# Attention probabilities of chunks 1 to 7 turned by DMA instead of TensorE

## Chip, cores and metric

One core of a Trainium2 chip runs the whole program. The metric is the device time of one execution in microseconds (us), as the median of several runs. A kernel is one launch; weights and inputs start in DRAM and the result ends in DRAM.

## The reference, cut to what matters

Attention over 4 batches x 8 heads (576 positions, 64 per head) feeds two feed-forward blocks one after the other. Four heads of a batch look at the last 32 positions, four at every 32nd position.

```python
scores = scale * q @ k.T                    # scale = 1/8
scores = where(mask[head], scores, -1e9)    # local heads: 0 <= q-k < 32; strided heads: q-k >= 0 and (q-k) % 32 == 0
attn = exp(scores - max(scores))
attn = attn / (sum(attn) + 1e-9)
x = (attn @ v), heads side by side          # 2304 tokens x 512
h = x @ moe_w_in;   x = (h * sigmoid(1.702 * h)) @ moe_w_out      # 512 -> 2048 -> 512
h = x @ moe2_w_in;  out = (h * sigmoid(h)) @ moe2_w_out
```

## The kernel before

**Order of work.** The engines' instruction streams are written out by a planner (class `Planner`, lines 62 to 180). Every piece of work is a task with a priority (a due time), an estimated cost for each engine that may do it, the tasks it follows and the buffers it takes. `Planner.run` plays the tasks through once at build time, giving each engine the ready task of lowest priority, and emits the instructions in that order. On the chip each engine then works through its own stream strictly in order, and waits where the plan was too early. A DMA task occupies SP for its issue; its data count as landed two us after a shared link, with 0.27 MB per us, has carried them (lines 171 to 173).

**Chunks.** The 2304 tokens are eight chunks of 288: a batch's first half (even chunks, `s = 0`) and second half (odd chunks, `s = 1`). `chunk(c)` (line 843) is the first feed-forward block: 16 tasks of 12 matmuls for `h` (line 862), then 16 of 12 for the output (line 893), each operand of chunks 1 to 7 being two fp16 parts, high and low, with three products for each pair. `attention(c, ...)` (line 565) is the attention of chunk c, and is planned into the feed-forward of chunk c-1: its tasks have due times between those of that chunk's matmuls, and the chunk's output `x1` must be ready when `chunk(c)` begins. Chunk 7's feed-forward and the second block follow in a second plan (lines 961 to 1334).

**Attention of one chunk.** `pair(i)`, i = 0 to 3 (line 632), does one local and one strided head. TensorE forms the scores with the queries on the partitions (line 669). VectorE takes the row maxima and subtracts them (678, 690), ScalarE takes the exponentials (698), VectorE the row sums and reciprocals (702, 715), and GpSimd multiplies (723), which leaves normalised fp32 probabilities: `sml`, 96 queries x 3 blocks x 128 keys, and `sms`, 72 x 4 x 72 in even chunks, 63 x 5 x 126 in odd ones. The product with V needs the keys on the partitions. TensorE transposes block by block into a PSUM bank (line 730: 3 blocks of `sml`, 4 or 5 of `sms`), then two evictions leave the two fp16 parts in `ptt`, scaled by `PSC` = 4096: the high part by ScalarE or VectorE (743, 745), the low part by VectorE (748). `times_v(pr)` (line 757) multiplies by V (780) for two heads at a time, in the order pr = 0, 2, 1, 3 (0 and 1 local, 2 and 3 strided), and lines 810 and 813 write `x1`. Chunk 0 works in fp32 and keeps one scaled fp32 copy in `ptt` (737).

**Buffers.** Eight PSUM banks (`ps`) serve everything; `sl` and `st` are four copies of `sml` and `sms`, `pt` six of `ptt`; `qh`, `vz` and `x1` exist once.

Of the kernel before, what the change touches and what calls it, by code (L numbers as in the profile page):

```python
# [22 lines left out]
PSC = 2.0 ** 12  # L23
# [160 lines left out]
def attention_moe_moe2_kernel(  # L184
# [146 lines left out]
    jk = at.tile([128, NK], BF16, name="jk")  # L331
    jv = at.tile([128, NK], BF16, name="jv")
# [23 lines left out]
    for i in range(2):  # L356
# [6 lines left out]
    nc.gpsimd.memset(vz[:, :, :, 1], 0.0)  # L363


    P = Planner({"ps": range(8), "rq": [0], "rk": range(2), "rv": [0], "qh": [0],
                 "k0": [0], "k1": [0], "vz": [0], "x1": [0], "sl": range(NSM), "st": range(NSM), "pt": range(NPT), "t": range(NTS),
# [6 lines left out]
    def act_t(n):  # L374
        return {"ACT": 0.17 + 0.00083 * n}
# [189 lines left out]
    def attention(c, b):  # L565
# [66 lines left out]
        def pair(i):  # L632
# [84 lines left out]

            for g in range(2):
# [3 lines left out]
                kno = P.add({"POOL": 0.25 + 0.0022 * nb * nk}, t + 8 + g, lambda on, g=g, smv=smv, nq=nq, nb=nb, nk=nk:  # L722
                            nc.gpsimd.tensor_tensor(  # L723
                                out=smv(), in0=smv(), in1=sus[0:nq, sl.idx, 3 * g:3 * g + nb, None].to_broadcast([nq, nb, nk]),
                                op=ALU.mult), [krc], (), [sl, st])
                p, pb = P.buf("ps"), P.buf("pt")
# [6 lines left out]
                if c == 0:  # L733
                    def evict(on, p=p, pb=pb, n=n, nk=nk):
                        o, x = ptt[0:nk, pb.idx].rearrange("p a n -> p (a n)").bitcast(F32)[:, 0:n], banks[p.idx][0:nk, 0:n]
                        if on == "ACT":
                            nc.scalar.activation(out=o, in_=x, func=AF.Copy, scale=PSC)
                        else:
                            nc.vector.tensor_scalar(out=o, in0=x, scalar1=PSC, scalar2=None, op0=ALU.mult)
                    kp = P.add({"DVE": 0.45} | act_t(n), t + 12 + g, evict, [ktr], [pb], [p])  # L740
                else:
                    kp = P.add(act_t(n) | {"DVE": 0.4}, t + 12 + g, lambda on, p=p, pb=pb, n=n, nk=nk:
# [14 lines left out]
        def times_v(pr):  # L757

            nq, nk, blocks = geom(s, pr >= 2)
            nb = len(blocks)  # L760
            t = b + tab["av"][pr % 2] + pr // 2
            pa = [P.buf("ps") for _ in range(1 if c else 2)]

# [639 lines left out]
```

## Time and profile before

| | |
|---|---|
| median of 3 runs | 878.31 us (874.52 to 879.46) |
| the profiled execution | 878.42 us, of which 876.6 us from its first to its last instruction |
| TensorE matmuls busy | 850.7 us (97% of the span) |
| VectorE / ScalarE / GpSimd busy | 694.1 / 537.5 / 417.3 us |
| chunks 1 to 7 of attention, with the feed-forward of chunks 0 to 6 around them | about 84 to 492 us of the span |

TensorE's matmuls overlap in the pipeline and their ends are modelled, so the cost of a group of matmuls in a stream is read as the distance from its start to the start of the next group, not as the sum of the durations. Idle time counts only on the engine that bounds a stretch. Lines such as L730 are lines of the kernel before.

### The profile page before, as it was taken

The numbers are of one execution on the slowest core, as the hardware profiler recorded it, in microseconds if no ns is written. First come the engines' busy times: TensorE is split into PE (matmuls) and PEld (weight loads), VectorE is DVE, ScalarE is ACT, GpSimd is POOL, SyncE is SP. The second block draws the span as 40 slices with busy tenths as digits, with TensorE's granted clock in tenths as the row PEclk, the third lists the DMA queues.
The fourth block names the chain that finished last, engine by engine and source line by source line (L and its number), as shares of the span: only waits on it lengthen the run. The fifth ranks groups of instructions, "written<-read, shape, count | busy, mean of one in ns | idle before, by whom it ended". The sixth has DMA issues, their size and how long they took to land.

```text
span 876.6 us, 21029 instructions
## 1 busy us (share of the span) xinstructions
PE 850.7 (97%) x8198; PEld 721.6 (82%) x8198; DVE 694.1 (79%) x1259; ACT 537.5 (61%) x1009; POOL 417.3 (48%) x432
## 2 busy tenths in 40 slices
PE   4999999899999999999999999999999999999997
PEld 3976768688888888878888888888888998888886
DVE  5769999989987799899577273789888799868742
ACT  5678568769869588697574334354555476646410
POOL 3657565554453465475323163677887552221110
PEclk9999999999999999999999999999999999999999
DMA  9948232268264375384300472576675898746501
GB/s 316 316 119 258 77 109 83 91 194 256 81 201 169 115 227 190 107 265 135 120 31 15 162 285 76 194 224 222 219 227 193 298 301 286 261 166 224 196 27 49
DMA packets 86083, 155.25 MB, mean 177 GB/s; under 512 B 8416, under 2 KB 45792, under 8 KB 84960
## 3 DMA queue, kind: packets, MB, share of 16 engines
q1 hardware_dynamic: 85984, 153.91, 53.6%
q8 instruction: 64, 1.05, 0.5%
q14 instruction: 35, 0.29, 0.1%
HBM read 100.40 MB, written 53.48 MB: 176 GB/s over the span
## 4 chain that ended last, share of the span: by engine, by line
PE 83%; DVE 9%; DMA 2%; issue 2%; POOL 1%; ACT 1%; SPq 0%; DVEq 0%; POOLq 0%
PE aps L1173 9%; PE aps L893 8%; PE aps L1284 8%; PE aps L862 7%; PE gps L893 5%; PE hps L1173 5%; PE gps L1173 4%; PE hps L1284 4%; PE gps L1284 4%; PE hps L893 3%; PE gps L862 3%; PE hps L862 3%; PE aps L859 2%; DMA tt<-g_scratch 2%; PE aps L669 2%
## 5 line engine op out<-in xcount | busy, mean ns | idle before, releaser
L1284 PEld LDWEIGHTS <-wf 128*128 128x128 f16 x1512 | 147.6, 98 | 19.5 <-issue 2.0
L1173 PEld LDWEIGHTS <-wf 128*128 128x128 f16 x1680 | 150.6, 98 | 15.3
L862 PEld LDWEIGHTS <-regA 128*128 128x128 f16 x1152 | 112.3, 98 | 28.7 <-issue 0.2
L893 PEld LDWEIGHTS <-regB 128*128 128x128 f16 x1152 | 108.5, 98 | 29.4 <-DVE sml L690 1.3
L989 POOL TENSOR_TENSOR tt<-tt 128x256 f32<-128x256 f32 (+2 forms) x84 | 74.7, 898 | 45.6 <-ACT tt L1185 13.4
L862 PE MATMUL aps<-x,regA 128*128 128x288 f16 x636 | 84.3, 286 | 0.0
L893 PE MATMUL aps<-g,regB 128*128 128x288 f16 x576 | 79.0, 289 | 1.7 <-DVE sml L690 1.2
L293 POOL TENSOR_TENSOR wm<-wm 128x512 int32<-128x512 int32 x32 | 45.8, 1430 | 60.9 <-DVE wm L288 47.1
L984 ACT ACTIVATE wf<-tt,xsg 128x512 f16<-128x512 f32 x87 | 58.0, 712 | 25.6 <-PE hps L1284 7.3
L996 DVE SCALAR_TENSOR_TENSOR wf<-tt,xsg,wf 128x512 f16<-128x512 f32 x87 | 71.4, 868 | 0.0
L723 POOL TENSOR_TENSOR sml<-sml,sus 96x384 f32<-96x384 f32 x32 | 30.3, 946 | 70.5 <-DVE sus L715 58.6
L1284 PE MATMUL aps<-regA,wf 128*128 128x256 f16 x456 | 53.2, 273 | 0.1
L1173 PE MATMUL aps<-xfa,wf 128*128 128x256 f16 (+1 forms) x528 | 53.1, 256 | 0.0
L893 PE MATMUL gps<-g,regB 128*128 128x288 f16 x336 | 45.7, 286 | 0.0
L1185 ACT ACTIVATE tt<-tt 128x512 f32<-128x512 f32 x39 | 24.4, 625 | 30.9 <-DVE tt L1180 29.5
L984 ACT ACTIVATE wf<-regB,xsg 128x512 f16<-128x512 f32 x39 | 26.8, 713 | 19.9 <-DMA regB<-g_scratch 7.4
L1173 PE MATMUL aps<-g,wf 128*128 128x256 f16 x324 | 38.8, 273 | 0.0
L1284 PE MATMUL aps<-regB,wf 128*128 128x256 f16 x312 | 37.0, 273 | 0.0
L862 PE MATMUL hps<-x,regA 128*128 128x288 f16 x264 | 35.6, 286 | 0.0
L723 POOL TENSOR_TENSOR sms<-sms,sus 72x288 f32<-72x288 f32 (+1 forms) x32 | 35.3, 1103 | 0.0
L862 PE MATMUL gps<-x,regA 128*128 128x288 f16 x252 | 34.2, 286 | 0.0
L1284 PE MATMUL hps<-regA,wf 128*128 128x256 f16 x264 | 32.4, 273 | 1.7 <-DVE x L1299 1.4
(350 smaller groups left out, 2098.1 us busy)
## 6 DMA issues: line engine op xcount, KB each, us to landing
tt<-g_scratch SPq DMA_DIRECT2D x76, 256.0 KB, 3.8
g_scratch<-tt SPq DMA_DIRECT2D x64, 256.0 KB, 3.0
w<-in_moe_w_out_dram SPq DMA_DIRECT2D x24, 512.0 KB, 4.3
rv<-in_v_dram SPq DMA_DIRECT2D x8, 1024.0 KB, 5.6
regB<-in_moe_w_in_dram SPq DMA_DIRECT2D x16, 512.0 KB, 8.8
w<-in_moe_w_in_dram SPq DMA_DIRECT2D x16, 512.0 KB, 3.7
w_scratch<-wm SPq DMA_DIRECT2D x32, 256.0 KB, 3.3
regB<-g_scratch SPq DMA_DIRECT2D x32, 256.0 KB, 3.8
```

The costliest lines, as they stand in the source:

```text
L293: nc.gpsimd.tensor_tensor(out=di, in0=m.bitcast(I32), in1=di, op=ALU.add)
L669: nc.tensor.matmul(x[0], lhsT=x[1], rhs=x[2], start=False, stop=x[3], skip_group_check=True)
L723: nc.gpsimd.tensor_tensor(out=smv(), in0=smv(), in1=sus[0:nq, sl.idx, 3 * g:3 * g + nb, None].to_broadcast([nq, nb, nk]), op=ALU.mult), [k ...
L859: nc.tensor.matmul(o, lhsT=w[:, kk, :], rhs=x1f[:, kk, :], start=(kk == 0), stop=(kk == KD - 1))
L862: nc.tensor.matmul(o, lhsT=pvA[:, f, x, kk, :], rhs=x1[:, y, kk, :], start=(i == 0), stop=(i == 3 * KD - 1))
L893: nc.tensor.matmul(o, lhsT=pvB[:, f, u, dt * 128:(dt + 1) * 128], rhs=g1[:, w, f, :], start=(f == 0 and j == 0), stop=(f == KF - 1 and j = ...
L984: nc.scalar.activation(out=out, in_=in_, func=AF.Copy, scale=s)
L989: return P.add({e: x for e, x in any_add(n).items() if e in by}, prio, lambda on: (nc.gpsimd if on == "POOL" else nc.vector).tensor_tensor ...
L996: dve_t(n), prio, lambda on: nc.vector.scalar_tensor_tensor(out=lo(), in0=src(), scalar=s(), in1=hi(), op0=ALU.mult, op1=ALU.subtract),
L1173: nc.tensor.matmul(place(b, f), lhsT=wf[:, nf * g + f, x, wa, 128 * kk:128 * kk + 128], rhs=rhs.rearrange("p (h t) -> p h t", h=2) if n2 = ...
L1185: return P.add(act_t(512), t + 5, lambda on: nc.scalar.activation(out=sl(b), in_=sl(b), func=AF.Silu), after, (), [b], tab="silu")
L1284: nc.tensor.matmul(bank(b)[:, 256 * half:256 * half + 256], lhsT=fb[:, x, a, 128 * f:128 * f + 128], rhs=wt[:, 4 * p + f, z, wi, :], start ...
```

## The change

For chunks 1 to 7, lines 723 to 750 are replaced. GpSimd first multiplies the reciprocals by `PSC` (one small instruction for each pair), then normalises as before. While the queries are still on the partitions, the high fp16 part is written by ScalarE or GpSimd and the low part, the difference, by VectorE or GpSimd, into `phl` (96 queries x 3 blocks x 2 parts x 128 columns) or `phs` (80 rows x 5 x 2 x 128). There is one buffer of each. Then one DMA transpose issued by SP for each of the two heads turns the whole buffer from SBUF to SBUF into `ptt`: 56 of them, 96 x 768 elements for a local head, 80 x 1024 or 64 x 1280 for a strided head (queries are rounded up to 16), 144 to 160 KiB each. The transposes on TensorE, their PSUM banks and both evictions fall away for these chunks. Chunk 0 keeps them. The layout of `ptt` and the slices that `times_v` reads are adapted. The targets `jk` and `jv` of the squares, whose contents nobody reads, become one byte wide, and `phs` is cleared once at the start by GpSimd.

```diff
-    NSM, NPT, NTS, NCV, NF = 4, 6, 4, 2, 8
+    NSM, NPT, NTS, NCV, NF, NHL = 4, 6, 4, 2, 8, 1
...
-    ptt = at.tile([128, NPT, 2, 316], F16, name="ptt")
+    ptt = at.tile([128, NPT, 640], F16, name="ptt")
+    phl = at.tile([LQ, NHL, NLB, 2, 128], F16, name="phl")
+    phs = at.tile([80, NHL, 5, 2, 128], F16, name="phs")
...
-    jk = at.tile([128, NK], BF16, name="jk")
-    jv = at.tile([128, NK], BF16, name="jv")
+    jk = at.tile([128, NK], mybir.dt.uint8, name="jk")
+    jv = at.tile([128, NK], mybir.dt.uint8, name="jv")
...
+    nc.gpsimd.memset(phs, 0.0)
...
+            kno = None
             for g in range(2):
...
-                kno = P.add({"POOL": 0.25 + 0.0022 * nb * nk}, t + 8 + g, ...
-                p, pb = P.buf("ps"), P.buf("pt")
+                def normalise(on, g=g, smv=smv, nq=nq, nb=nb, nk=nk):
+                    if c and g == 0:
+                        nc.gpsimd.tensor_scalar(out=sus[:, sl.idx, 0:n8], in0=sus[:, sl.idx, 0:n8], scalar1=PSC, scalar2=1.0,
+                                                op0=ALU.mult, op1=ALU.mult)
+                    nc.gpsimd.tensor_tensor(
+                        out=smv(), in0=smv(), in1=sus[0:nq, sl.idx, 3 * g:3 * g + nb, None].to_broadcast([nq, nb, nk]),
+                        op=ALU.mult)
+                kno = P.add({"POOL": (0.25 if c == 0 or g else 0.45) + 0.0022 * nb * nk}, t + 8 + g, normalise,
+                            [krc, *([kno] if c else [])], (), [sl, st])
+                pb = P.buf("pt")
+                if c:
+                    hb = P.buf("hs" if g else "hl")
+                    n = nb * nk
+                    ph = lambda z, ...: (phs if g else phl)[0:nq, hb.idx, 0:nb, z, 0:nk]
+                    kh_ = P.add(any_hi(n), t + 9 + g, lambda on, ph=ph, smv=smv: put(on, ph(0), smv(), 1.0), [kno], [hb], [sl, st])
+                    kl_ = P.add({"POOL": 0.25 + 0.0022 * n} | dve_t(n), t + 9.5 + g, lambda on, ph=ph, smv=smv: (
+                        nc.gpsimd if on == "POOL" else nc.vector).tensor_tensor(out=ph(1), in0=smv(), in1=ph(0), op=ALU.subtract),
+                        [kh_], (), [sl, st, hb], two=True)
+
+                    def turn(on, g=g, nq=nq, nb=nb, hb=hb, pb=pb):
+                        m = -(-nq // 16) * 16
+                        nc.sync.dma_start_transpose(
+                            ptt[:, pb.idx, 0:2 * nb * m].rearrange("p (b q) -> p b q", q=m),
+                            (phs if g else phl)[0:m, hb.idx, 0:nb].rearrange("p b z k -> p (b z k)"))
+                    kp = P.add({"SP": 1.2}, t + 10 + g, turn, [kl_], [pb], [hb], wait=("dma", 0.15))
+                    pts[i + 4 * g] = (kp, pb)
+                    continue
+                p = P.buf("ps")
...  (the transposes and the fp32 eviction stay for chunk 0; lines 742 to 750 are gone)
-                                rhs=ptt[0:nk, pb.idx, z, r],
+                                rhs=ptt[0:nk, pb.idx, (2 * i + z) * nr + done - q0:(2 * i + z) * nr + nq],
```

## Rows read from the trace of the kernel before

**Rows 1.** The page: busy time, share of the span and instructions of each engine.
```profile
PE 850.7 (97%) x8198; PEld 721.6 (82%) x8198; DVE 694.1 (79%) x1259; ACT 537.5 (61%) x1009; POOL 417.3 (48%) x432
```

**Rows 2.** Stretches of the span: length, busy us (instructions) by engine, clock, DMA.
```profile
84.00:131.00 47.00, 44.04 (x330) 33.39 (x331) 45.00 (x84) 30.04 (x52) 29.55 (x25) 1.00 0.36 115
167.00:190.00 23.00, 22.41 (x257) 19.00 (x255) 20.77 (x53) 14.77 (x38) 11.91 (x13) 1.00 0.37 119
190.00:492.00 302.00, 302.00 (x3241) 248.37 (x3240) 250.95 (x521) 219.61 (x442) 133.53 (x123) 1.00 0.46 145
```

**Rows 3.** Timeline of TensorE around chunk 3's attention: start, us, line, count.
```profile
229.71 1.64 PE L893 MATMUL hps<-g,regB 128*128 128x288 f16 x12
231.29 0.51 PE L730 MATMUL aps<-idt,sms 63*126 63x63 f32 x5
231.73 1.64 PE L893 MATMUL aps<-g,regB 128*128 128x288 f16 x12
...
237.07 1.64 PE L893 MATMUL aps<-g,regB 128*128 128x288 f16 x12
238.55 0.41 PE L730 MATMUL gps<-idt,sml 96*128 96x96 f32 x3
238.80 1.64 PE L893 MATMUL aps<-g,regB 128*128 128x288 f16 x12
...
247.21 0.51 PE L730 MATMUL aps<-idt,sms 63*126 63x63 f32 x5
...
251.37 1.02 PE L780 MATMUL aps<-ptt,vz 126*128 126x63 f16 x30
252.24 1.63 PE L893 MATMUL aps<-g,regB 128*128 128x288 f16 x12
...
256.22 1.64 PE L862 MATMUL aps<-x,regA 128*128 128x288 f16 x12
```

**Rows 4.** Timeline of TensorE in chunk 4's attention, with blocks of 72.
```profile
287.96 0.42 PE L730 MATMUL aps<-idt,sms 72*72 72x72 f32 x4
288.21 1.64 PE L893 MATMUL gps<-g,regB 128*128 128x288 f16 x12
```

**Rows 5.** Busy time of single lines from 84 to 492: L730, then L748.
```profile
84.00:492.00 408.00, 24.51 (x212) 19.81 (x212) 1.00 0.43 136
...
84.00:492.00 408.00, 24.85 (x56) 1.00 0.43 136
```

**Rows 6.** Groups by shape from 190 to 492, GpSimd: multiplications and conversions.
```profile
L507 POOL TENSOR_TENSOR wm<-wm 128x256 f32<-128x256 f32 x25 | 21.1, 862 | 10.6 <-DMA wm<-w_scratch 7.1 <-ACT g L385 2.4 <-DVE wm L507 0.4
L723 POOL TENSOR_TENSOR sml<-sml,sus 96x384 f32<-96x384 f32 x20 | 20.4, 1020 | 52.1 <-DVE sus L715 40.8 <-ACT g L385 5.4 <-ACT ptt L743 4.8
```

**Rows 7.** Groups by shape, VectorE from 205 to 490, ScalarE from 90 to 450.
```profile
L690 DVE TENSOR_TENSOR sml<-aps,nms 96x384 f32<-96x384 f32 x12 | 6.5, 541 | 0.0
...
L385 ACT ACTIVATE wm<-wm,s 128x512 f16<-128x512 f32 x8 | 5.7, 718 | 1.1 <-POOL wm L507 0.9
```

**Rows 8.** The page: DMA queue, then issues with KB and median us to landing.
```profile
q1 hardware_dynamic: 85984, 153.91, 53.6%
...
rv<-in_v_dram SPq DMA_DIRECT2D x8, 1024.0 KB, 5.6
```

**Rows 9.** All DMA issues, of 144 KB; then one line's SP issue, ns min/median/max.
```profile
x_scratch<-ts SPq DMA_DIRECT2D x28, 144.0 KB, 1.9
...
L839 SPq DMA_DIRECT2D x_scratch<-ts x28: 319/324/455, 129.9 to 492.4; - x28
```

**Rows 10.** Timeline of SP's queue in chunk 3's attention.
```profile
241.09 0.32 SPq L839 DMA_DIRECT2D x_scratch<-ts  x1
```

**Rows 11.** Timeline of TensorE at the end of chunk 7's attention.
```profile
482.26 0.52 PE L730 MATMUL gps<-idt,sms 63*126 63x63 f32 x5
...
486.43 1.02 PE L780 MATMUL gps<-ptt,vz 126*128 126x63 f16 x30
487.29 4.57 PE L893 MATMUL aps<-g,regB 128*128 128x288 f16 x36
```

More of the change, by code (lines that the diff above doesn't have):

```diff
@@ L363, in attention_moe_moe2_kernel @@
     nc.gpsimd.memset(vz[:, :, :, 1], 0.0)
+    nc.gpsimd.memset(phs, 0.0)
     P = Planner({"ps": range(8), "rq": [0], "rk": range(2), "rv": [0], "qh": [0],
-                 "k0": [0], "k1": [0], "vz": [0], "x1": [0], "sl": range(NSM), "st": range(NSM), "pt": range(NPT), "t": range(NTS),
+                 "k0": [0], "k1": [0], "vz": [0], "x1": [0], "sl": range(NSM), "st": range(NSM), "pt": range(NPT), "hl": range(NHL), "hs": range(NHL), "t": range(NTS),
                  "cv": range(NCV), "f": range(NF)} | {f"g{f}": [0] for f in range(KF)}, 0.27)
@@ L721, in pair @@
                 smv = lambda g=g, nk=nk: probs(g, sl, st, s)[:, :, 0:nk]
[L722 to L725, printed above, removed]
-                p, pb = P.buf("ps"), P.buf("pt")
+                def normalise(on, g=g, smv=smv, nq=nq, nb=nb, nk=nk):
[5 more added lines that the diff above has]
+                        op=ALU.mult)
@@ new lines, in pair @@
+                kno = P.add({"POOL": (0.25 if c == 0 or g else 0.45) + 0.0022 * nb * nk}, t + 8 + g, normalise,
[4 more added lines that the diff above has]
+                    n = nb * nk
+                    ph = lambda z, g=g, nq=nq, nb=nb, nk=nk, hb=hb: (phs if g else phl)[0:nq, hb.idx, 0:nb, z, 0:nk]
+                    kh_ = P.add(any_hi(n), t + 9 + g, lambda on, ph=ph, smv=smv: put(on, ph(0), smv(), 1.0), [kno], [hb], [sl, st])
[10 more added lines that the diff above has]
+                    continue
@@ L732, in pair, with evict @@
                 n = nb * nq
[L733 to L742, printed above, removed]
-                               nc.scalar.activation(out=ptt[0:nk, pb.idx, 0, 0:n], in_=banks[p.idx][0:nk, 0:n], func=AF.Copy, scale=PSC)
-                               if on == "ACT" else
-                               nc.vector.tensor_scalar(out=ptt[0:nk, pb.idx, 0, 0:n], in0=banks[p.idx][0:nk, 0:n], scalar1=PSC,
-                                                       scalar2=None, op0=ALU.mult),
-                               [ktr], [pb], [p])
-                    kp = P.add({"DVE": 0.42}, t + 13 + g, lambda on, p=p, pb=pb, n=n, nk=nk: nc.vector.scalar_tensor_tensor(
-                        out=ptt[0:nk, pb.idx, 1, 0:n], in0=banks[p.idx][0:nk, 0:n], scalar=PSC, in1=ptt[0:nk, pb.idx, 0, 0:n],
-                        op0=ALU.mult, op1=ALU.subtract), [kp], (), [p, pb])
+                def evict(on, p=p, pb=pb, n=n, nk=nk):
+                    o, x = ptt[0:nk, pb.idx].bitcast(F32)[:, 0:n], banks[p.idx][0:nk, 0:n]
+                    if on == "ACT":
+                        nc.scalar.activation(out=o, in_=x, func=AF.Copy, scale=PSC)
+                    else:
+                        nc.vector.tensor_scalar(out=o, in0=x, scalar1=PSC, scalar2=None, op0=ALU.mult)
+                kp = P.add({"DVE": 0.45} | act_t(n), t + 12 + g, evict, [ktr], [pb], [p])
                 pts[i + 4 * g] = (kp, pb)
@@ L759, in times_v @@
             nq, nk, blocks = geom(s, pr >= 2)
-            nb = len(blocks)
+            nb, nr = len(blocks), -(-nq // 16) * 16
             t = b + tab["av"][pr % 2] + pr // 2
@@ L775, in mm @@
                                 lhsT=rv.rearrange("p b h d -> p b (h d)")[0:nk, vb, 128 * (pr % 2):128 * (pr % 2) + 128],
-                                rhs=ptt[0:nk, pb.idx].rearrange("p a n -> p (a n)").bitcast(F32)[:, r],
+                                rhs=ptt[0:nk, pb.idx].bitcast(F32)[:, r],
                                 start=True, stop=True)
```

## Prediction, written before the changed kernel was run

> **What bounds the kernel now.** I read the busy times of the page first: TensorE's matmuls cover 97% of the span, VectorE 79%, GpSimd 48% [rows 1]. An average over stages proves little, so next come the stretches in which the edited attention runs. From 190 to 492 us, attention of chunks 3 to 7, TensorE is busy for 302.00 of 302.00 us, VectorE for 250.95 and GpSimd for 133.53, at the full clock [rows 2]: time taken from TensorE's stream there shortens the run as long as nothing else arrives late. Chunk 2 (167 to 190) is nearly the same, 22.41 of 23.00 us. Chunk 1 (84 to 131) is another case: TensorE 44.04 of 47.00 us, VectorE 45.00, so VectorE is the tighter of the two. Last I read TensorE's stream around the transposes, because its busy figures overlap: what a group costs is the distance to the next start.
>
> **What is removed from TensorE.** Three local blocks start at 238.55 and the next matmuls at 238.80, 0.25 us [rows 3]. Five strided blocks of an odd chunk start at 231.29, the next at 231.73, 0.44 us; and the twelve matmuls ahead of them run from 229.71 to 231.29, 1.58 us, where the twelve ahead of the local blocks, from 237.07 to 238.55, take 1.48: 0.10 more, which I count to the transposes, so 0.54. Four strided blocks of an even chunk cost 0.25 us [rows 4]. Chunks 1 to 7 have 28 pairs, 16 of them in the four odd chunks: 28 x 0.25 + 16 x 0.54 + 12 x 0.25 = 18.6 us for 212 transposes, whose summed busy time, 24.51 us, is more because they overlap [rows 5]. By stretch: chunks 3 to 7 give 20 x 0.25 + 12 x 0.54 + 8 x 0.25 = 13.5 us, chunk 2 gives 4 x 0.50 = 2.0, chunk 1 gives 4 x 0.79 = 3.2. The first two count in full. Of chunk 1 I count half, 1.6, as VectorE is as full there; the bounds are 0 and 3.2. Gain: 17.1 us.
>
> **What moves on the other engines.** VectorE loses the 56 low parts, 24.85 us [rows 5], and 9 high parts; ScalarE loses 47. They come back with the queries on the partitions, 384 elements a row instead of 288, or 288 and 630 instead of 288 and 315. A high part on ScalarE is near its 512-element conversion, 718 ns [rows 7]. A low part on VectorE is near the subtraction of 384 elements, 541 ns, so about 0.44 to 0.85 us by shape; on GpSimd, which 44% of the stretch keeps busy, it is near the multiplication of the same shape, 1020 ns, or, by elements, the 862 ns for 256 (1.3 us) [rows 6]. All 56 on VectorE would be 28 x 0.54 + 16 x 0.85 + 12 x 0.44 = 34.0 us against 24.85 + 9 x 0.44 = 28.8: at worst 5 us more in 372, at best 29 us less. Either fits where VectorE has 51 us of room, from 190 to 492, and I put it at 0 there. GpSimd's small multiplication of the reciprocals, 28 times, is hidden: GpSimd waits 40.8 us for reciprocals alone from 190 to 492 [rows 6]. Clearing `phs` is one instruction ahead of everything; I count 0, at most 1 us. The one-byte squares write fewer bytes in the same number of elements; I see neither gain nor loss above 0.1 us each, on engines with room. The 56 PSUM banks that come free can only help, by an unknown amount that I leave at 0.
>
> **What is added: 56 DMA transposes on SP's queue.** No row shows one. From below: an ordinary 144 KB store lands 1.9 us after its issue, and SP spends 324 ns on that issue [rows 9]. From above, I price pieces. The queue's 85984 packets took 53.6% of 16 engines for 876.6 us [rows 8], 87 ns each. A local head is read as 96 x 6 = 576 rows of 256 bytes: 576 x 87 / 16 = 3.1 us; a strided one as 640, 3.5 us. If the written side, 128 partitions x 6 to 10 blocks, comes on top and does not overlap, it is 7.3 us local and 9.1 to 10.5 strided. I take 3 to 4 us from issue to landing, nearest to the store of the same size, and about 1 us on SP, three ordinary issues' worth, since one instruction holds 6 to 10 groups of 128 columns; the bounds are 0.32 us and 10 x 0.32 = 3.2. Eight transposes a chunk then hold the link for some 8 x 1 to 8 x 3.3 = 8 to 26 us of the 302 / 5 = 60 us that a chunk takes, and SP for 8.
>
> A transpose waits on SP for its low part. Queued behind it are weight loads, the stores of finished output (241.09) [rows 10] and the next chunk's loads of q, k and v, of which v takes 5.6 us [rows 8]. The first two feed work in the background; q, k and v are issued half a chunk ahead. I count 0.
>
> At one place the Trainium skill speaks against the change. The row says that TensorE turns three 96-column blocks in 0.25 us inside this stream [rows 3]. The Trainium skill, VectorE: DVE Perf Modes, section The three transpose paths, gives 390 ns on TensorE and 1309 ns on the crossbar for a 128 x 128 bf16 block, and advises TensorE where a PSUM destination will do. TensorE's figure is over four times this trace's; if the crossbar's were paid for every block, an estimate from that page is 16 x 1.309 = 20.9 us a pair in odd chunks and 18.3 in even ones, 555 us in all, and the run would end near 1030 us. The Trainium skill, DMA: Bandwidth & Descriptors, section Latency and other measured facts, has an effective 261 GB/s for DMA transposes instead, by which 147,456 bytes take an estimated 0.6 us, and the forecast stands. No run here shows either yet.
>
> **The latency and where it hurts.** Today the last strided transposes of chunk 3 start at 247.21 and the product that needs them at 251.37 [rows 3]. The new path, high part 0.7, low part 0.6 to 1.3, issue and landing 3 to 4, some 0.2 us of signals, is 4.5 to 6.2 us against about 1.5 (transposes, eviction, low part): 3 to 4.7 us later. One buffer of each kind makes the next pair's high part wait for this landing: 4.5 to 6.2 us a pair, and pairs come about 5 us apart, so the last pair may slip 1 to 3 us more. Cover: after the last product there is a group of L893 at 252.24, then the next chunk's scores, and `h` of the next chunk starts at 256.22, with one more group of L893 behind it; the plan can pull up more of the next scores. At the end of chunk 7 the cover is thinner: the product at 486.43 is followed by three groups from 487.29 on [rows 11], 4.4 us, and no further attention. I charge 1.5 us at that end and 0.3 at each of five other boundaries: 3.0 us, with bounds 0 and, if nothing covers, some 2.5 x 7 = 17.
>
> **The sum.** The profiled execution took 878.4 us (876.6 of span), 0.1 above the median of three. 878.4 - 13.5 - 2.0 - 1.6 + 3.0 = 864.3 us; I say 864. Its own range: chunk 1 worth 0 or 3.2, latency 0 to 8, reach from 859 to 871.
>
> **Rivals.**
> 1. *Late transposes take the place of the removed ones.* A product with V stands in TensorE's stream where the plan expected the landing; if it lands later TensorE stands still, other ready matmuls or not. With 3.3 us of link for each transpose, 8 x 3.3 = 26 us barely fit into the 25 us in which four pairs come, and they share the link with v and the weights. At 1.5 to 3.5 us for each of seven chunks this costs 10 to 25 us: 872 to 886, centre 878. For it: one buffer, a strict order, a forecast landing nobody has measured. Against it: the planner counts the landing and orders by it, and TensorE's other work is plentiful until the end of a chunk.
> 2. *The transpose itself bounds, slower than before.* If read and write pieces are paid one after the other, a pair costs 7.3 + 10.5 us of queue in odd chunks, 7.3 + 9.1 in even ones: 16 x 17.8 + 12 x 16.4 = 482 us against the 408 us that this part takes now. The run ends at about 878 + 74 + 10 of start-up, 960. It decides from about 3.5 us of queue for each transpose, above which eight no longer fit beside the pairs; each further us costs up to 56 us. The page's 1309 ns a block is of this kind. For it: elements of two bytes change partition. Against it: an ordinary transfer of the size needs 1.9 us.
> 3. *More than the matmuls.* VectorE, rid of up to 29 us, and the free banks also shorten chunks 1 and 2, where TensorE idles 3.6 us: 852 to 858.
> 4. *It does not do what it says.* A DMA transpose that still uses TensorE or a second copy is excluded by the diff; a chunk that is bound by VectorE throughout, so that no gain shows, by the 302.00 of 302.00 [rows 2].
>
> **Chances.** Forecast 0.55; rival 1 0.24 (0.06 of it faster by over 0.5%, 0.12 within, 0.06 slower); rival 2 0.15; rival 3 0.06. About 0.5% is what a measurement of this kernel can tell from no change: 873.9 to 882.7 us. Faster 0.55 + 0.06 + 0.06 = 0.67, within 0.12, slower 0.06 + 0.15 = 0.21. The range takes the forecast, rival 1 and the near end of rival 3: 857 to 886, and leaves out rival 2.
>
> **What would show it.** Right: no L730 after chunk 0; between 190 and 480 us TensorE still near 100% with the next chunk's `h` about 2 to 3 us closer to the last one; transposes landing in 3 to 4 us; the second plan beginning about 14 us earlier. Rival 1: idle time of TensorE before L780 or L862 whose releaser is a DMA into `ptt`, or ScalarE or VectorE behind it. Rival 2: landings beyond 6 us, SP busy issuing or `phl` refills waiting on DMA, a low clock where TensorE stands. Wrong at once: transposes whose landing depends on the loads of q, k and v in front of them, or GpSimd's low parts far over 1.3 us, so that VectorE's and GpSimd's streams hold up the exponentials.

## The result, and the profile after

The changed kernel takes 883.59 us (median of 11 runs, 878.57 to 889.08), the kernel before in the same session 877.67 us (11 runs, 872.54 to 879.51): a ratio of 1.0073, with an interval of 1.0050 to 1.0096. The forecast of 864 us had the wrong sign. The profiled execution of the changed kernel took 885.19 us, 883.4 of them span, against 878.42 and 876.6 before.

The page of the changed kernel, first the busy times that answer to [rows 1], then the DMA packets and the two transposes with their median us to landing:

```profile
PE 838.1 (95%) x7986; PEld 709.9 (80%) x7986; DVE 698.0 (79%) x1217; ACT 545.4 (62%) x1008; POOL 470.5 (53%) x508
...
DMA packets 121922, 163.95 MB, mean 186 GB/s; under 512 B 44256, under 2 KB 81632, under 8 KB 120800
...
ptt<-phl SPq DMA_TRANSPOSE x28, 2.8
ptt<-phs SPq DMA_TRANSPOSE x28, 2.9
```

TensorE lost its 212 transposes and 12.6 us of busy time. VectorE was not relieved (694.1 to 698.0), GpSimd got 53 us more (417.3 to 470.5). The transposes themselves are as cheap as forecast. Where the time went is read from stretches of the span (length, busy us and instructions of PE, PEld, DVE, ACT and POOL, then clock, DMA share, GB/s); the first and the last answer to [rows 2]:

```profile
84.00:131.00 47.00, 38.92 (x277) 30.33 (x276) 43.97 (x72) 28.19 (x47) 32.52 (x30) 0.95 0.50 133
131.00:150.00 19.00, 12.18 (x170) 9.99 (x171) 14.83 (x27) 13.07 (x27) 10.29 (x10) 0.86 0.37 93
150.00:190.00 40.00, 37.23 (x336) 29.25 (x336) 36.29 (x70) 34.02 (x66) 22.92 (x27) 0.96 0.38 107
190.00:492.00 302.00, 292.09 (x3070) 238.63 (x3068) 260.28 (x503) 224.64 (x447) 179.69 (x187) 0.99 0.64 172
```

The two stretches between them in the kernel before:

```profile
131.00:150.00 19.00, 18.95 (x187) 15.28 (x185) 17.77 (x33) 17.10 (x38) 10.03 (x11) 1.00 0.33 99
150.00:190.00 40.00, 35.90 (x409) 29.58 (x408) 36.55 (x80) 27.01 (x61) 20.51 (x21) 0.96 0.35 117
```

In chunk 1's stretch TensorE falls from 44.04 to 38.92 busy us of 47, and in the 19 us behind it from 18.95 to 12.18, at a granted clock of 0.86 for 1.00. That 0.86 is a mean of two levels: behind TensorE's idle time from 126.60 to 132.55 us the granted clock was 0.50 (1.2 GHz), and from 137 to 144 us 1.00 (2.4 GHz):

```profile
133.00:136.00 3.00, 3.00 (x10) 0.50 0.33 49
```

TensorE, never idle from 190 to 492 us before, now stands there for 9.9 us. By the starts of each chunk's `h`, the changed kernel is 9.2 us late in chunk 1 (141.5 for 132.3) and 17.8 in chunk 2 (212.1 for 194.3), and wins ten back by the start of the second plan (499.4 for 491.7).

**An account for TensorE.** For the stretch from 79.2 us (the second half of chunk 0) to the first matmul of the second plan, one row each: of the kernel before, of the changed kernel, and of the runs below with chunks 3 to 7 alone, chunk 1 alone, chunks 2 to 7, and chunks 3 to 7 with earlier scores.

```profile
79.20:491.70 412.50, 404.43 (x4202) 328.95 (x4200) 355.07 (x722) 298.43 (x596) 197.69 (x180) 1.00 0.43 138
```

```profile
79.20:499.40 420.20, 392.13 (x3994) 317.50 (x3993) 361.96 (x681) 305.78 (x595) 249.72 (x256) 0.98 0.58 156
```

```profile
79.20:489.40 410.20, 394.23 (x4049) 319.12 (x4048) 356.34 (x684) 307.26 (x605) 235.33 (x231) 0.99 0.55 154
```

```profile
79.20:503.30 424.10, 404.73 (x4174) 329.31 (x4173) 358.04 (x711) 306.77 (x608) 200.32 (x189) 0.98 0.44 137
```

```profile
79.20:492.90 413.70, 391.45 (x4023) 316.40 (x4022) 365.26 (x687) 301.61 (x589) 245.63 (x249) 1.00 0.59 156
```

```profile
79.20:488.90 409.70, 392.93 (x4051) 318.08 (x4050) 360.70 (x679) 302.73 (x600) 242.55 (x242) 1.00 0.54 154
```

Length less busy time is idle time. What a lower clock cost is busy time x (1 - clock), summed over pieces of 5 us of the same view. The rest is work, and its fall is what the removed transposes gave (us; the clock has two digits and the pieces begin anew at each chunk's `h`, so a figure is good to about 0.5):

| by DMA | length | idle | clock | rest | saved | forecast as saved |
|---|---|---|---|---|---|---|
| none (before) | 412.5 | 8.1 | 1.7 | 402.7 | | |
| 1 to 7 (the change) | 420.2 | 28.1 | 6.1 | 386.0 | 16.7 | 18.7 |
| 3 to 7 | 410.2 | 16.0 | 2.9 | 391.3 | 11.4 | 13.5 |
| 1 | 424.1 | 19.4 | 4.5 | 400.2 | 2.5 | 3.2 |
| 2 to 7 | 413.7 | 22.3 | 1.7 | 389.7 | 13.0 | 15.5 |
| 3 to 7, scores earlier | 409.7 | 16.8 | 1.7 | 391.2 | 11.5 | 13.5 |

The change saved TensorE 16.7 us of work, gave it 20.0 us of new idle time and 4.4 of lower clock: 7.7 us longer. Of these 24.4 us, 17.7 lie ahead of chunk 2's `h` (27.5 there, 9.8 before). What TensorE waited for from 84 to 215 us (total, times, longest):

```profile
PE gps L301 <- POOL regB L293: 8.0, 2, 6.0
PE gps L879 <- DVE g L395: 6.4, 3, 5.5
PE aps L797 <- DMA ptt<-phl: 3.1, 1, 3.1
```

The two long waits are not for transposes: the sums of the first block's second weight matrix (L301) wait for GpSimd's conversion of its last piece (L293), and chunk 1's `h` waits for VectorE's low part of `g` (L395), which reads the PSUM bank that `h` writes next.

### The profile page after: what moved, and what is told of

It reads as the page before. It is cut to its first block, busy times and chain, and to the rows that moved or that the text cites. A ratio compares the mean times of both kernels' runs of the same rounds, so it can differ in the third digit from the quotient of the medians.

```text
span 883.4 us, 20755 instructions
## 1 busy us (share of the span) xinstructions
PE 838.1 (95%) x7986; PEld 709.9 (80%) x7986; DVE 698.0 (79%) x1217; ACT 545.4 (62%) x1008; POOL 470.5 (53%) x508
## 2 busy tenths in 40 slices
DMA packets 121922, 163.95 MB, mean 186 GB/s; under 512 B 44256, under 2 KB 81632, under 8 KB 120800
## 3 DMA queue, kind: packets, MB, share of 16 engines
q8 instruction: 62, 1.02, 0.5%
## 4 chain that ended last, share of the span: by engine, by line
PE 63%; DVE 16%; POOL 5%; ACT 5%; DMA 5%; issue 5%; SPq 0%; DVEq 0%; POOLq 0%; ACTq 0%
PE aps L1190 9%; PE aps L1301 8%; PE hps L1190 5%; PE gps L1190 4%; PE aps L879 4%; PE hps L1301 4%; PE gps L1301 4%; PE aps L910 3%; PE gps L879 3%; PE hps L910 2%; DMA ptt<-phl 2%; PE hps L879 2%; PE gps L910 2%; DVE wf L1013 2%; PE aps L876 2%
## 5 line engine op out<-in xcount | busy, mean ns | idle before, releaser
L910 PEld LDWEIGHTS <-regB 128*128 128x128 f16 x1152 | 110.7, 99 | 29.0 <-issue 0.7
L879 PE MATMUL aps<-x,regA 128*128 128x288 f16 x552 | 73.4, 286 | 0.8 <-DVE g L395 0.7
L293 POOL TENSOR_TENSOR wm<-wm 128x512 int32<-128x512 int32 x32 | 44.1, 1380 | 36.0 <-DVE wm L288 33.2
L910 PE MATMUL hps<-g,regB 128*128 128x288 f16 x384 | 51.8, 290 | 0.5 <-DVE g L395 0.5
L879 PE MATMUL gps<-x,regA 128*128 128x288 f16 x324 | 45.3, 292 | 6.4 <-DVE g L395 6.4
L910 PE MATMUL aps<-g,regB 128*128 128x288 f16 x384 | 50.9, 286 | 0.0
L910 PE MATMUL gps<-g,regB 128*128 128x288 f16 x384 | 50.8, 286 | 0.0
L1202 ACT ACTIVATE tt<-tt 128x512 f32<-128x512 f32 x39 | 24.4, 625 | 29.4 <-DVE tt L1197 29.3
L729 POOL TENSOR_SCALAR sus<-sus 96x8 f32<-96x8 f32 (+1 forms) x28 | 11.4, 406 | 54.4 <-DVE sus L718 48.9
L731 POOL TENSOR_TENSOR sml<-sml,sus 96x384 f32<-96x384 f32 x32 | 30.9, 965 | 14.7 <-DVE sus L718 12.4
```

What stands on the lines that cost most here:

```text
L293: nc.gpsimd.tensor_tensor(out=di, in0=m.bitcast(I32), in1=di, op=ALU.add)
L729: nc.gpsimd.tensor_scalar(out=sus[:, sl.idx, 0:n8], in0=sus[:, sl.idx, 0:n8], scalar1=PSC, scalar2=1.0, op0=ALU.mult, op1=ALU.mult)
L731: nc.gpsimd.tensor_tensor(out=smv(), in0=smv(), in1=sus[0:nq, sl.idx, 3 * g:3 * g + nb, None].to_broadcast([nq, nb, nk]), op=ALU.mult)
L879: nc.tensor.matmul(o, lhsT=pvA[:, f, x, kk, :], rhs=x1[:, y, kk, :], start=(i == 0), stop=(i == 3 * KD - 1))
L910: nc.tensor.matmul(o, lhsT=pvB[:, f, u, dt * 128:(dt + 1) * 128], rhs=g1[:, w, f, :], start=(f == 0 and j == 0), stop=(f == KF - 1 and j = ...
L1202: return P.add(act_t(512), t + 5, lambda on: nc.scalar.activation(out=sl(b), in_=sl(b), func=AF.Silu), after, (), [b], tab="silu")
```

## Experiments

In the experiments' diffs `c` is the chunk; where the DMA route is not taken, lines 730 to 750 of the kernel before stand in its place, writing into the new layout of `ptt`. `...` marks lines left out. Runs of different rows were made in several sessions, so each ratio is to the kernel before in the same session.

### Which chunks lose

Theory P keeps the prediction's gain for chunks 3 to 7 and has chunks 1 and 2 lose, where VectorE and GpSimd also convert and split the weights. Rival L was that late transposes eat part of the gain everywhere. The first run takes the DMA route for chunks 3 to 7 only, the second for 1 and 2, the third for 1, the fourth for 2 to 7.

```diff
...                              (the same condition at the multiplication of the reciprocals)
-                if c:
+                if c > 2:        # second run: 0 < c < 3; third: c == 1; fourth: c > 1
...
```

> The new route for chunks 3 to 7 alone; chunks 1 and 2 keep the transposes on TensorE and the two evictions (written into the new layout of ptt). Theory P (the loss sits in chunks 1 and 2, where VectorE and GpSimd also convert and split the weights; in the traces the feed-forward of chunk 1 begins 9.2 us late, that of chunk 2 17.8 us, and by the start of chunk 7's 10 of these are won back): about 868 us, 10 below before, and the feed-forward of chunk 3 begins where it does before, near 256 us. Rival L (late landing and the single buffer cost something in every chunk): 5.4 of the 8.7 us that TensorE waits for ptt lie in chunks 3 to 7, and stay; 875 to 880 us.

> The new route for chunks 1 and 2 alone; chunks 3 to 7 keep the transposes on TensorE. Theory P: slower than before by about what the traces show at the start of chunk 2's feed-forward, 12 to 18 us, 890 to 896 us, so slower than the changed kernel too. Rival L (a cost in every chunk alike): 16 pairs fewer on the new route, so between the two kernels, 877 to 881 us.

> Chunk 1 alone by DMA, chunks 2 to 7 with TensorE's transposes. Chunks 1 and 2 together cost 14 us; chunk 1 begins its `h` 9 us late in the full change, chunk 2 another 8.6. Theory 1 (each of the two chunks pays for itself): 883 to 887, 7 to 10 us slower than before, `h` of chunk 1 at 139 to 143. Theory 2 (chunk 1's delay breaks chunk 2's work, which would be cheap alone): 888 to 892, nearly the whole 14.

> Chunks 2 to 7 by DMA, chunk 1 with TensorE's transposes. Theory 1 (chunk 1 pays by itself, the rest gains): chunk 1 alone cost 12 to 13 us and the full change 6, so chunks 2 to 7 alone should end at about 871 (869 to 874), below chunks 3 to 7 alone at 872.9, and `h` of chunk 1 starts at 132. Theory 2 (chunk 2 loses 8 us more, as its `h` in the full change lags by 17.8 us against 9.2 in chunk 1): 878 to 883.

| by DMA | us (runs) | ratio to before, interval | `h` of chunk 1, chunk 2, second plan |
|---|---|---|---|
| none | 876.7 to 878.6 in the three sessions | | 132.3, 194.3, 491.7 |
| 3 to 7 | 872.93 (10) | 0.9968 (0.9941 to 0.9995) | 132.2, 194.2, 489.4 |
| 1 and 2 | 890.62 (4) | 1.0172 (1.0143 to 1.0202) | 136.4, 206.7, 501.8 |
| 1 | 890.55 (4) | 1.0152 (1.0120 to 1.0185) | 141.5, 203.4, 503.3 |
| 2 to 7 | 876.98 (10) | 1.0011 (0.9992 to 1.0030) | 132.6, 199.8, 492.9 |

Chunk 1 alone costs 12 to 13 us, more than the whole change. Theory P holds in sign for both parts, but the 868 us it gave chunks 3 to 7 was missed, and their 3.8 us lie between P and L. Nor do the parts add up: 12 + 3 to 4 (chunk 2: 876.98 less 872.93) - 4 would be 889, and the change took 883.6. Chunk 2 costs nothing that can be told from noise where chunk 1 is already late (1.0172 for 1.0152), and about 4 us where it isn't. The third run met its second theory's number, though chunk 2 is not cheap alone; the fourth fell between its two. TensorE's waits in chunk 1 with chunk 1 alone are those of the full change, for L301 in the same line as above and for `h`:

```profile
PE gps L896 <- DVE g L395: 6.4, 3, 5.5
```

Why GpSimd converts so late is in its timeline (start, us, instructions, idle time before them and its releaser), with VectorE's step ahead of the last conversion (L288). Before:

```profile
119.39 2.17 POOL L293 TENSOR_TENSOR regB<-wm,regB 128x512 int32<-128x512 int32 x1 [0.78 <-DVE wm L288]
...
122.21 1.27 POOL L293 TENSOR_TENSOR regB<-wm,regB 128x512 int32<-128x512 int32 x1
...
121.08 0.69 DVE L288 SCALAR_TENSOR_TENSOR wm<-w,aps 128x512 int32<-128x512 int32 x1
```

In the changed kernel, with three instructions of VectorE:

```profile
119.26 2.48 POOL L293 TENSOR_TENSOR regB<-wm,regB 128x512 int32<-128x512 int32 x2
125.05 1.85 POOL L390 TENSOR_SCALAR regA<-regA,s 128x512 f16<-128x512 f32 x1 [3.31 <-DVE regA L395]
...
128.99 1.23 POOL L731 TENSOR_TENSOR sms<-sms,sus 63x630 f32<-63x630 f32 x1
130.18 2.31 POOL L293 TENSOR_TENSOR regB<-wm,regB 128x512 int32<-128x512 int32 x1
...
119.27 3.14 DVE L743 TENSOR_TENSOR phs<-sms,phs 63x630 f16<-63x630 f32 x1
...
124.87 0.19 DVE L718 RECIPROCAL sus<-sus 96x8 f32<-96x8 f32 x1
...
126.99 0.69 DVE L288 SCALAR_TENSOR_TENSOR wm<-w,aps 128x512 int32<-128x512 int32 x1
```

A strided low part takes VectorE 3.14 us beside GpSimd's conversions. Behind it on VectorE stand low parts of weights, the sums and the reciprocals of the next pair (124.87). GpSimd idles 3.31 us for VectorE, then writes the high part of a block of weights, normalises that pair and writes its local high part, and only then converts the last piece of the second weight matrix, at 130.18 in place of 122.21. VectorE's own step for that piece (L288) runs 5.9 us later too, at 126.99 for 121.08; GpSimd's order adds the other 2.1. The chain of waits, followed back, goes through the same low part (`phs`), the pair's normalisation and this conversion.

The scale of these weights, which the second half of the feed-forward needs, is ready at 136.38 (`inv`, L266) where it was at 129.02.

### What GpSimd's and VectorE's added work costs

One kernel takes the added work off GpSimd: ScalarE writes the high part with the factor, VectorE the low part, the reciprocals are not multiplied. Theory G: GpSimd's added work is the loss; theory V: VectorE's is.

```diff
-                        nc.gpsimd.tensor_scalar(out=sus[:, sl.idx, 0:n8], ...)
...
-                    kh_ = P.add(any_hi(n), ...: put(on, ph(0), smv(), 1.0), ...
-                    kl_ = P.add({"POOL": 0.25 + 0.0022 * n} | dve_t(n), ... .tensor_tensor(out=ph(1), in0=smv(), in1=ph(0), op=ALU.subtract),
+                    kh_ = P.add({"ACT": any_hi(n)["ACT"]}, ...: put(on, ph(0), smv(), PSC), ...
+                    kl_ = P.add(dve_t(n), ... nc.vector.scalar_tensor_tensor(
+                        out=ph(1), in0=smv(), scalar=PSC, in1=ph(0), op0=ALU.mult, op1=ALU.subtract),
```

> All of chunks 1 to 7 on the new route, but GpSimd does what it did before: the multiplication of the reciprocals falls away, ScalarE writes every high part with the factor 4096, VectorE every low part in one instruction with that factor. Theory G (GpSimd's added work, 53 us, is the cause: its instructions stand in one order, the addition that the sum of squares on TensorE waits for behind the pair's work, 8.0 us of waiting in chunk 1): GpSimd falls back to about 417 us busy, those waits go, 868 to 875 us. Rival V (the low part from two operands in SBUF on VectorE is the cause: 1.04 us for 384 elements and 1.26 for 630 by the median of after, against 0.45 from PSUM): 56 of them take some 62 us instead of 28, and VectorE is later than in the changed kernel: 886 us or more.

877.61 us, ratio 1.0023 (1.0008 to 1.0039): about 5 us better than the change, each against the kernel before of its session, with neither theory's numbers met. All 56 low parts took VectorE 43.3 us, not the 62 that theory V counted. TensorE's waits from 84 to 215 us:

```profile
PE aps L794 <- DMA ptt<-phl: 8.8, 1, 8.8
PE gps L301 <- POOL regB L293: 3.0, 4, 1.1
```

The waits for GpSimd fall from 8.0 to 3.0 us, and chunk 1 has another: its product with V stands 8.8 us for the last local transpose, and `h` starts at 144.3. Up to chunk 2's `h`, idle time and lower clock together are 27.5 us in the change, 23.3 here and 9.8 before (by the account above): some 4 of the relief's 5 us lie there, and 13.5 more than before remain. Nothing covers a late product in chunk 1: before, `h` of chunk 1 begins at 132.31, right behind it. But of the 8.8 us only the end is the transpose's. Issued at 135.05, it landed 2.5 us later; its low part took 0.54 us, but ran only at 134.44, as VectorE's stream was late: that pair's reciprocals came at 130.17, where the kernel before has them at 123.95:

```profile
130.17 0.19 DVE L718 RECIPROCAL sus<-sus 96x8 f32<-96x8 f32 x1
...
134.44 0.54 DVE L739 SCALAR_TENSOR_TENSOR phl<-sml,phl 96x384 f16<-96x384 f32 x1
...
135.05 1.20 SPq L745 DMA_TRANSPOSE ptt<-phl  x1
```

The edit also gives ScalarE and VectorE the work and changes the order of all streams, so its 5 us are a net figure and no price of GpSimd's work alone.

The same relief restricted to chunks 2 to 7 and to 3 to 7:

> ScalarE writes the high parts and VectorE the low ones, GpSimd as before, on the new route for chunks 2 to 7 alone; chunk 1 keeps TensorE. With the run for chunks 3 to 7 below it gives chunk 2's price by itself. Theory C (no cover: chunk 1's products with V come last ahead of its feed-forward, 130.62 to 132.31 us in the trace of before, so each us of lateness stops TensorE, while chunk 2's have groups of L893 behind them): chunk 2 costs within 2 us of nothing, some 866 to 868 us. Rival W (VectorE's load in both chunks, by the splits of the weights, is the cause): chunk 2 costs 5 us or more, 870 to 874 us.

> The same for chunks 3 to 7 alone; chunks 1 and 2 keep TensorE. In the trace of e4 the feed-forward of chunk 2 begins 14.4 us late and the second plan only 0.6: 13.8 us were won in chunks 3 to 7, the 13.5 that the removed matmuls take there. Theory G2 (with GpSimd as before the gain of chunks 3 to 7 comes whole): 878 - 13 = 863 to 867 us. Rival L (late landings and one buffer take part of it whatever the engines do, as in e1, where TensorE waited 5.8 us for ptt): 871 to 875 us.

876.31 us, ratio 0.9994 (0.9967 to 1.0021), and 874.79 us, ratio 0.9972 (0.9957 to 0.9987). Without the relief the same chunks took 876.98 and 872.93: from chunk 2 on it brings nothing. The first run missed both its numbers; of the second's, G2's fell and L's was met.

One step was measured by itself, in instructions added behind the end of the kernel before: the low part of 96 x 384 on VectorE with its fp32 operand in SBUF or in PSUM, alone and beside a multiplication of the same shape on GpSimd.

```diff
...
+    for src in (f[0], bk):           # SBUF, then PSUM
+        for _ in range(12):
+            low(src, h[1])           # scalar_tensor_tensor, as L748
...
+    pool_mul(12)                     # GpSimd alone
+    for src in (f[0], bk):           # both engines
...
+        pool_mul(12)
+        for _ in range(14):
+            low(src, h[2])
...
```

> The kernel before, and behind its last product a measurement alone: a low part on VectorE (96 x 384, fp32 and fp16 in, fp16 out), twelve times with the fp32 operand in SBUF, twelve with it in PSUM, then GpSimd's fp32 multiplication of 96 x 384 twelve times, then the low parts of both kinds again while GpSimd multiplies. The time of the run says nothing. Theory S (two operands in SBUF and GpSimd's accesses hold each other up): 0.54 us alone, 1.0 us or more beside GpSimd with the operand in SBUF, unchanged, about 0.45 to 0.55, with it in PSUM. Rival (the longer low parts in the changed kernel are a matter of the form, fp16 beside fp32): the same duration alone and beside GpSimd.

Timeline of this run's end (`tt` in SBUF, `hps` in PSUM):

```profile
876.95 7.01 DVE L1341 SCALAR_TENSOR_TENSOR xfa<-tt,xfa 96x384 f16<-96x384 f32 x12
884.00 7.02 DVE L1341 SCALAR_TENSOR_TENSOR xfa<-hps,xfa 96x384 f16<-96x384 f32 x12
...
891.74 10.74 POOL L1345 TENSOR_TENSOR tt<-tt 96x384 f32<-96x384 f32 x12
...
902.58 13.10 POOL L1345 TENSOR_TENSOR tt<-tt 96x384 f32<-96x384 f32 x12
...
903.46 13.81 DVE L1341 SCALAR_TENSOR_TENSOR xfa<-tt,xfa 96x384 f16<-96x384 f32 x14
...
918.12 10.74 POOL L1345 TENSOR_TENSOR tt<-tt 96x384 f32<-96x384 f32 x12
...
918.99 8.19 DVE L1341 SCALAR_TENSOR_TENSOR xfa<-hps,xfa 96x384 f16<-96x384 f32 x14
```

Alone both cost 0.58 us. Beside GpSimd the low part with two operands in SBUF takes 13.81 / 14 = 0.99 us and GpSimd's instruction 1.09 for 0.90; from PSUM neither is touched (0.585 and 0.90). Theory S, in which two SBUF operands and GpSimd hold each other up, is confirmed for this form. The old low part read PSUM, the new one reads SBUF.

The changed kernel's low part is another instruction (a plain subtraction), but its own trace shows the same:

```profile
373.86 0.54 DVE L743 TENSOR_TENSOR phl<-sml,phl 96x384 f16<-96x384 f32 x1
...
258.28 1.59 DVE L743 TENSOR_TENSOR phl<-sml,phl 96x384 f16<-96x384 f32 x1
```

Of the 15 local low parts on VectorE, five took 0.52 to 0.56 us and ten 0.94 to 1.66; beside each of the ten GpSimd ran a multiplication, a conversion or a low part of two operands (beside one of the five, too). A strided one of 63 x 630 took 0.80 us with GpSimd idle (at 492.99) and the five others 0.89 to 3.14 beside it; one of 72 x 288 took 0.44 with GpSimd idle. By these figures, an estimate, the 23 would have cost VectorE about 13 us in place of 28 without GpSimd.

### Is it the plan's order?

The planner's cost of the low parts set to about what they took:

```diff
-                    kl_ = P.add({"POOL": 0.25 + 0.0022 * n} | dve_t(n), ...
+                    kl_ = P.add({"POOL": 0.2 + 0.0018 * n, "DVE": 0.55 + 0.00125 * n}, ...
```

> The changed kernel with one edit: the planner counts a low part at what the trace of after shows (VectorE 0.55 + 0.00125 n, GpSimd 0.2 + 0.0018 n us) and not at 0.12 + 0.00112 n and 0.25 + 0.0022 n. The work is the same, only its order and its split between the two engines change. Theory O (the order is the cause: VectorE's stream runs later than the plan thought): 870 to 876 us. Theory P or V (the work itself is the cause, in any order): within 3 us of the changed kernel, 881 to 887 us.

883.06 us, ratio 1.0096 (1.0067 to 1.0126): no gain over the change. Theory O's number was missed, that of P and V met: counting the low parts rightly does not by itself help the planner. Other orders are not ruled out by it.

The second test has the last four conversions of the second weight matrix due 8 us earlier, in the changed kernel and, as a control, in the kernel before:

```diff
-        t = WOUT0 + WOUTS * i
+        t = WOUT0 + WOUTS * i - (8 if i >= 12 else 0)
```

> The full change, and the last four conversions of the second weight matrix with their Gram products are due 8 us earlier, so that GpSimd and VectorE take them ahead of the attention's added work in chunk 1. Theory K (in chunk 1 GpSimd's last conversion of weights, ended at 132.5 in place of 123.5 us, holds up TensorE's Gram product, the scale and with it the second half of the feed-forward): the waits of 6 and 5.5 us go, and the time falls by 5 to 10 us, to 873 to 878. Theory A (VectorE is full there, so what goes ahead of it only delays chunk 1's probabilities and its product with V): 881 to 886.

> The kernel before with the same four conversions due 8 us earlier, the control of the run with the full change. Both theories: they are early enough before, 876 to 880; if it gains over 2 us, as much of the other run's gain is not the change's.

882.11 us, ratio 1.0073 (1.0047 to 1.0098), and 883.18 us for the control, ratio 1.0076 (1.0048 to 1.0103). Theory K's number was missed, and the wait for GpSimd stays:

```profile
PE gps L301 <- POOL regB L293: 8.5, 2, 6.4
```

GpSimd did convert the last piece earlier (124.21 for 130.18), but TensorE came to the sums earlier too (120.19 for 126.60), as the new plan runs what lies ahead of both sooner. Theory A's number held, but this does not show its reason. The control, for which 876 to 880 had been expected, is the more telling: with no work changed at all, an order shifted in one place costs 6 us. Differences of a few us between two plans are therefore no price of a single instruction. And against this control the changed kernel is no slower (882.11 for 883.18): that the change loses 6 us holds for the order it was put into, not for every order.

### The waits for transposes

In chunks 3 to 7 alone, 11.4 us were saved and 7.9 came back as idle time, 5.8 of it for transposes:

```profile
PE gps L814 <- DMA ptt<-phl: 4.4, 3, 2.1
PE aps L814 <- DMA ptt<-phl: 1.4, 2, 1.0
```

Three ways to get rid of them were tried on that kernel (872.93 us): to let the planner count the landing later, to give `phl` a second buffer (and `ptt` four for six), and to make the scores due earlier, the last one with a control on the kernel before.

```diff
-                    kp = P.add({"SP": 1.2}, t + 10 + g, turn, [kl_], [pb], [hb], wait=("dma", 0.15))
+                    kp = P.add({"SP": 1.2}, t + 10 + g, turn, [kl_], [pb], [hb], wait=5.0)
```

> Chunks 3 to 7 by DMA as in the run that had only these (872.9 us, where TensorE stood 5.8 us for transposes), but the planner counts a transpose as landed 5.1 us after SP has issued it, in place of two us after its share of the link (about 2.6 us). Theory O (the products with V stand too early in TensorE's order, and other matmuls could go ahead of them): TensorE's waits for `ptt` fall below 2 us and the time to 867 to 870. Theory B (at the end of a chunk nothing else is left to go ahead, so the wait only moves to the next chunk's `h`): waits for `ptt` fall too, but the time stays at 871 to 876.

```diff
-    NSM, NPT, NTS, NCV, NF, NHL = 4, 6, 4, 2, 8, 1
+    NSM, NPT, NTS, NCV, NF, NHL = 4, 4, 4, 2, 8, 1
-    phl = at.tile([LQ, NHL, NLB, 2, 128], F16, name="phl")
+    phl = at.tile([LQ, 2, NLB, 2, 128], F16, name="phl")
```

> Chunks 3 to 7 by DMA, with two buffers `phl` in place of one; the room comes from `ptt`, four buffers in place of six. Theory W (the single buffer makes the chain late: GpSimd and ScalarE waited some 4.6 us for a transpose to have read `phl`): TensorE's waits for `ptt` fall from 5.8 to under 3 us and the time to 868 to 871. Theory N (the buffer is not what ends last; the high and low parts, issue and landing are): waits of 5 to 7 us remain, 871 to 875.

```diff
-        tab = ATT0 if c == 0 else ATT1 if c == 1 else ATT
+        tab = ATT0 if c == 0 else ATT1 if c == 1 else ATT if c == 2 else ATT | {"s": 18.0}
```

> Chunks 3 to 7 by DMA, and the scores of these chunks are due 4 us earlier (18 in place of 22), so that the longer way to `ptt` begins sooner; the products with V keep their due times. In the run with chunks 3 to 7 alone, TensorE's matmuls fell by 11 us of time from 79 us to the second plan, and 8 us of new waits and 1 us of lower clock took most of it back. Theory L (these waits are the longer latency, which more lead covers): waits for `ptt` fall below 2 us, the time to 866 to 870. Theory V (what waits is a strict order against VectorE's lateness, of which the transposes are one case; scores pulled ahead delay conversions as much): 871 to 877.

> The control: the kernel before with the scores of chunks 3 to 7 due 4 us earlier. TensorE is never idle there from 190 to 492 us, so earlier scores can win nothing: both theories 876 to 881. A change of over 3 us would be that of the order alone.

| | us (runs) | ratio, interval | idle of TensorE, 79.2 us to the second plan |
|---|---|---|---|
| landing counted later | 888.16 (4) | 1.0126 (1.0097 to 1.0154) | 26.1 |
| two buffers `phl` | 877.94 (10) | 1.0003 (0.9984 to 1.0023) | 18.1 |
| scores 4 us earlier | 871.50 (10) | 0.9956 (0.9932 to 0.9981) | 16.8 |
| the control | 876.32 (10) | 0.9989 (0.9965 to 1.0013) | 8.9 |

Counting the landing later costs about 14 us by the ratios, and both theories were wrong: the waits for transposes rise from 5.8 to 10.6 us, most of them now for the strided ones.

```profile
PE aps L814 <- DMA ptt<-phs: 6.0, 2, 3.9
PE hps L814 <- DMA ptt<-phs: 3.3, 1, 3.3
```

A second `phl` lowers the waits for transposes to 3.0 us, nearly as theory W had it, but the time missed both theories: about 3 us slower by the ratios (one new wait, for `x` from VectorE, is 3.2 us); fewer buffers `ptt` are mixed in, so this speaks only against a gain, not on the buffer by itself. Earlier scores lower the waits for transposes from 5.8 to 3.6 us, but others come (the longest 2.2), and idle time stays about the same, 16.8 for 16.0:

```profile
PE aps L672 <- DVE qh L395: 2.2, 1, 2.2
PE aps L814 <- DMA ptt<-phs: 2.1, 2, 1.7
PE gps L814 <- DMA ptt<-phl: 1.5, 1, 1.5
```

Theory V held in number, and the new waits are for VectorE as it said. At 871.50 us this is the fastest of all, 0.4% below before; it does not differ from the 872.93 of the same chunks beyond their intervals.

## Why the prediction was wrong, step by step

**What TensorE is rid of: right.** 18.7 us in all chunks were worked out from the distances between starts; 16.7 were measured, 11.4 of 13.5 from chunk 3 on.

**The transposes' price: right in the median, save for what stands ahead of them.** 2.8 and 2.9 us to landing were forecast as 3 to 4, and 1.2 us on SP as about 1. The 35,839 packets that came on top (86,083 to 121,922) are 640 a transpose; 576 and 640 rows had been counted. The Trainium skill, VectorE: DVE Perf Modes, section The three transpose paths, was weighed with 1309 ns a block: a local head, six blocks in 2.8 us, shows no such price. But "Queued behind it are weight loads [...] I count 0" was looked at from one side only. The 56 landings range from 2.5 to 6.8 us, and of the nine of 4.5 us or more, eight were issued within 4 us behind a load of an input from DRAM (of the other 47, fourteen). In chunk 2 a transpose stands right behind the next chunk's `k` on SP:

```profile
199.46 0.60 SPq L559 DMA_DIRECT2D rk<-in_k_dram  x1
200.16 1.22 SPq L748 DMA_TRANSPOSE ptt<-phl  x1
```

In the chain it lands after 5.87 us, and TensorE stands 3.1 us for it:

```profile
200.16 5.87 DMA ptt<-phl
```

"Transposes whose landing depends on the loads [...] in front of them" was in the list of what would prove the forecast wrong. That the loads delayed this one is read from the order on SP; no run moved them.

**The other engines at 0, and chunk 1 with nothing to lose: the step that failed.** The added work of VectorE and GpSimd was put at 0 from 190 to 492 us, where VectorE has room, and has no term at all ahead of that, in chunks 1 and 2; and chunk 1's own term was bounded by 0 and 3.2 us of gain. The runs showed 24.4 us of new idle time and lower clock instead, 17.7 of them ahead of chunk 2's `h`, and chunk 1 alone 12 to 13 us slower. Groups by shape in the changed kernel, 84 to 492 us (busy us, mean ns of one, idle time before them):

```profile
L743 DVE TENSOR_TENSOR phl<-sml,phl 96x384 f16<-96x384 f32 x15 | 15.3, 1022 | 1.6 <-POOL phl L390 0.8 <-ACT phl L388 0.7
L743 POOL TENSOR_TENSOR phs<-sms,phs 63x630 f16<-63x630 f32 x10 | 13.8, 1380 | 1.4 <-ACT phs L388 1.1
L743 POOL TENSOR_TENSOR phl<-sml,phl 96x384 f16<-96x384 f32 x13 | 11.9, 916 | 0.1
L743 DVE TENSOR_TENSOR phs<-sms,phs 63x630 f16<-63x630 f32 x5 | 9.0, 1805 | 0.7 <-ACT phs L388 0.7
```

The prediction priced a low part on VectorE at 0.54 and 0.85 us, by a subtraction that reads one operand (`aps`) from PSUM [rows 7]; they took 1.02 and 1.81. GpSimd's, priced 1.02 to 1.3, took 0.92 and 1.38. 23 low parts cost VectorE 28.0 us (the two rows above and three of 72 x 288), as much as the 28.8 that 56 low and 9 high parts did. The price by shape was right for a low part alone (0.52 to 0.56 and 0.80 us, above); that both operands now lie in SBUF, beside an engine that gets 53 us busier, was not asked.

**Chunk 1: the term with the largest error.** It was a gain of 1.6 us with bounds 0 and 3.2, and it was a loss of 12 to 13. The prediction read that VectorE is full there (45.00 of 47.00, [rows 2]) and concluded that a gain would not show; it did not conclude that added work shows as a loss there. It did not ask what else hangs on VectorE and GpSimd: the conversion of the weights and their scale. The loss is placed in chunk 1 by its own run, and the waits name the two engines. How it splits between them, and between work and order, stays open: the relief gains a net 5 us, VectorE's stream is late without GpSimd's added work too, and an order shifted in one place costs the kernel before as much.

**The latency: 3.0 us with bounds 0 and 17.** In the full change TensorE waits 8.7 us for transposes, in chunks 2 to 6 alone, within the bounds and three times the value. The end of chunk 7, charged with half of it, costs nothing. The cover was read at the end of chunks 3 and 7; chunk 1 has none, which shows in the relieved kernel.

**The rivals.** The range 857 to 886 holds the time only by rival 1 (872 to 886), and that is luck: its mechanism, late transposes, is 8.7 of 20.0 us of new idle time. The other way to lose that was weighed, rival 2, was the transpose too dear, and it did not happen. The real one, a loss in chunk 1 where VectorE is full, was no rival; GpSimd's low parts holding up other streams were only in the last sentence.

**What stays open.** Why chunk 2 costs 4 us alone and nothing behind a late chunk 1 was not settled. The runs don't split the 7.9 us of new idle time in chunks 3 to 7 further: it changes its place with each shift of the order, and none of the three attempts made it smaller. Whether another order would let the whole change win is untested.

## What to carry to other kernels

Time taken off the bounding engine is won only where every other input still comes in time: read each stretch, the fullest first, and ask what else its busy engines feed. When elementwise work moves from PSUM to two SBUF operands, price it beside GpSimd, not by its shape. In a kernel whose streams are planned as a whole, run the same shift of order on the kernel before as a control: here it alone moved the time by 6 us, as much as the change did.

## What the runs showed of the hardware

A low part on VectorE with both operands in SBUF and a multiplication on GpSimd slow each other (0.58 to 0.99 us, 0.90 to 1.09), and one operand in PSUM avoids it (0.585 and 0.90). The Trainium skill, SBUF — State Buffer, section SBUF: two separate sides, says that a VectorE instruction with two SBUF inputs and a GpSimd one that reads SBUF exclude each other for their whole length. The trace agrees on which operands matter, not on the size: one after the other, 14 x 0.585 + 12 x 0.895 us would be 18.9, and both were done in 14.7 us (902.58 to 917.27).

A DMA transpose of 144 KB from SBUF to SBUF lands in 2.8 us (median of 28) and holds SP's queue for 1.2 us, where a store of that size took 1.9 and 0.3 [rows 9].
